# Long convolution by FFT and phase mixing on one core: an inverse table kept on chip by mirror symmetry, a filter spectrum stored once and read doubled, and the phases cut into half tiles, 16 of 44 woven into the last group

## Chip, cores and metric

One core of one Trainium2 chip. The metric is the device time of one execution in microseconds (us), the median of several. All runs told here may be compared. They were made in rounds, on several chips of the machine, and in each round the kernel before ran too. The granted TensorE clock is given as a share of full speed.

## The reference

```python
# x (8, 5696, 128), h (5696, 128), all float32
def _attn_ref(x, h):                       # causal long convolution along the sequence
    L = 2 * S
    y = irfft(rfft(x, n=L, axis=1) * rfft(h, n=L, axis=0)[None], n=L, axis=1)[:, :S]
def _moe_ref(x, w_theta, w_tok_r, w_tok_i, w_ch):   # its x is y of above
    theta = x @ w_theta
    zr, zi = x * cos(theta), x * sin(theta)
    y = einsum('ts,bsd->btd', w_tok_r, zr) + einsum('ts,bsd->btd', w_tok_i, zi)
    u = x + y
    return u + maximum(u @ w_ch, 0)
```

## The kernel before

The FFT of length 11392 is split as 178 x 64. An *evacuation* is the copy of matmul results out of PSUM, the memory into which TensorE accumulates, by VectorE or ScalarE. The program has these parts, in order:

- *Set-up*: trigonometric tables, and the spectrum of h, which goes to HBM. The table of the inverse's last step goes to HBM too.
- *Eight groups* (four pairs of batches, two halves of the 128 channels). Each group has a *middle stage* (C, first inverse step, with A, the first forward step of the next group, interleaved), and then a *forward/inverse stage* (B of the next group interleaved with D of this one). B multiplies by the spectrum of h in 12 chunks; each chunk loads one tile `hs` of 256 KB. Three of these stages (after groups 0, 2 and 4) also load new x, 5.8 MB. The last group has no next one, so its last stage is D alone.
- *Phases*: 22 tiles of 128 tokens, each with theta, sine (made in a tile `red`), cosine (in a tile `mag`) and five stores: one of y, two of zr, two of zi. They load the transposed result back as `ya`.
- *Token pass*: the large matmuls, about 1650 us. The change leaves it alone.

```python
hf_hbm = nc.dram_tensor("hf_hbm", (2, 2 * NCK, P, 2, HD * CK), F16, ...)    # P = 128 rows: every row of 64 twice
e_hbm = nc.dram_tensor("e_hbm", (K1, N2, 2, NB), F16, ...)
fh = pool("fft_h", 3)
# ... set-up: spectrum stored twice (e = 0, 1); seven chunks of the inverse table made and written to e_hbm ...

def stage_b(a_of, dh):                      # forward, second step, and product with the spectrum
    def chunk(c):
        hs = fh.tile([P, 2, HD * CK], F16, tag="hs", name="hs")
        nc.sync.dma_start(hs, hf_hbm[dh, c])
        ps = f2(a_of, c)
        xs = fs.tile([P, 2, HD, CK], F16, tag="xs", name="xs")
        nc.scalar.activation(xs[:, :, :, :ck], ps, AF.Copy)
        for r in range(2):
            nc.vector.tensor_tensor(uv[r][...], xs[...], hv[:, r:r + 1, ...].to_broadcast(...), op=mult)

def stage_c(st):                            # inverse, first step: 16 matmuls a chunk, then
    ...
        nc.vector.tensor_copy(st["g"][...], ps[...])

def stage_d(st, bp, dh):                    # inverse, last step
    def chunk(n0, cn):
        et = fs.tile([P, CN, 2, NB], F16, tag="et", name="et")
        nc.sync.dma_start(et[:K1, :cn], e_hbm[:, n0:n0 + cn, :, :])
        ...
                nc.tensor.matmul(o, g_[:K1, ri * N2 + n0 + j, :], et[:K1, j, ri, :], ...)
        nc.scalar.activation(yt[...], ps[...], AF.Copy)

for g, (bp, dh) in enumerate(groups):
    st = {}
    nxt, a_of = front(g + 1) if g + 1 < len(groups) else ([], None)
    woven(stage_c(st), nxt)
    if dh == 0 and bp + 1 < B // 2:
        x16s[bp + 1] = load_x(bp + 1)
    woven(stage_b(a_of, groups[g + 1][1]) if nxt else [], stage_d(st, bp, dh))

# phases: pool of red and mag with bufs=4; eight loads of ya; then 22 times
#   8 transposes, copies to y_ap (half VectorE, half ScalarE), store of y_ap,
#   theta by matmuls, Abs, Sin, Sin on ScalarE (1024 wide), two products on VectorE,
#   four stores of zr and zi:
        for r, (z, dst) in enumerate(((zr, zr_hbm), (zi, zi_hbm))):
            for e in range(2):
                ...
                nc.sync.dma_start(dst[p_, t0 // 64, i, :, b0 * D:b0 * D + n], z[e * 64:e * 64 + 64])
```

## Time and profile before

Two runs: 2367.80 and 2369.16 us, median 2368.48. The table is read from the trace. "Gap" is the time from the end of a middle stage's last evacuation (1.2 us after its start) to the start of the next middle stage's first one: that is the forward/inverse stage.

| Part | us |
|---|---|
| first middle stage's first evacuation at | 131.5 |
| gaps with x (three) | 39.3, 39.8, 39.3 |
| gaps without x (three), and the last | 28.1, 25.9, 25.0, 24.6 |
| last middle stage's first evacuation at | 562.4 |
| from there to the last phase tile on ScalarE (705.0) | 142.6 |
| rest, the token pass | about 1658 |

The windows view gives busy times by stage. Its columns are the window, its length, then busy us and instruction count of TensorE, its weight loads, VectorE, ScalarE and GpSimd, then the granted TensorE clock, the DMA share (of 16 engines; that it comes out a little over 1 in one row shows that it is rough) and GB/s. The rows are a middle stage, a gap with x, a gap without, the last inverse stage, the wait for ya, and the phases.

```profile
core 0: us, PE busy (x) PEld busy (x) DVE busy (x) ACT busy (x) POOL busy (x), PEclk, DMA share, GB/s
128.00:161.00 33.00, 32.34 (x419) 32.09 (x420) 21.06 (x19) 12.14 (x16) 0.31 (x1) 0.93 0.09 25
161.00:199.00 38.00, 15.66 (x465) 14.18 (x465) 14.51 (x24) 16.63 (x20) 1.84 (x4) 0.71 0.94 213
231.00:256.00 25.00, 15.93 (x457) 14.43 (x455) 14.35 (x24) 16.58 (x20) 0.00 (x0) 0.72 0.78 216
581.00:603.00 22.00, 11.08 (x129) 9.39 (x126) 5.45 (x13) 6.14 (x8) 13.95 (x27) 0.50 1.12 184
603.00:626.00 23.00, 6.49 (x53) 4.41 (x52) 0.42 (x1) 0.29 (x1) 0.00 (x0) 0.61 0.95 238
626.00:709.00 83.00, 54.26 (x577) 38.69 (x574) 68.65 (x84) 77.25 (x88) 0.00 (x0) 0.92 0.90 267
```

The middle stage is TensorE's (32.3 of 33 us). In both gaps no engine is busy for more than 17 us, while the DMA share is 0.78 to 0.94: loads bound them. In the phases ScalarE is busy 77 of 83 us.

The waits view of the eight groups (us in total, times, longest) names those loads: the spectrum tile hs and the inverse table et.

```profile
DVE u_t L274 <- DMA hs<-hf_hbm: 87.5, 36, 16.5
PE ps L305 <- DMA et<-e_hbm: 75.8, 28, 11.1
```

The DMA view of a gap without x (232 to 254 us): GB/s in 40 slices, and the issue line (count, size, median us from issue to landing).

```profile
GB/s 0 117 188 265 140 217 364 275 177 252 322 297 243 198 163 178 201 156 197 276 145 244 150 118 355 333 256 149 30 45 160 264 111 149 293 256 318 198 315 319
hs<-hf_hbm SPq DMA_DIRECT2D x10, 256.0 KB, 4.2
```

An hs of 256 KB landed in 4.2 us while et and the stores of yt ran beside it, and the rate moved mostly between 110 and 360 GB/s.

### The profile page before, as it was taken

Reading aid. Unit: us, or ns where it says so; the run is one execution under the profiler, and the core shown is the slowest. Engines: PE = TensorE matmul, PEld = TensorE weight load, DVE = VectorE, ACT = ScalarE, POOL = GpSimd, SP = SyncE. Lnnn points to the kernel's source line nnn. Section 1 sums busy time; section 2 is a strip of 40 time slices with the busy share of each in tenths; the row PEclk is TensorE's granted clock in tenths of the full one; section 3 lists DMA queues with packets and bytes.
Section 4 is the critical chain, followed back from the end, with each engine's and each line's share of the span. In section 5 each row is a group of like instructions: output and inputs, shape, how many; then the busy total and the mean of one; then the engine's idle time right before and its main releaser. Section 6 shows DMA issues by size and latency. Waiting matters only on the chain.

```text
span 2363.4 us, 42201 instructions
## 1 busy us (share of the span) xinstructions
PE 2068.5 (88%) x16255; PEld 1184.1 (50%) x16255; DVE 1671.0 (71%) x2943; ACT 641.9 (27%) x895; POOL 841.2 (36%) x1527
## 2 busy tenths in 40 slices
PE   3367868686567999999999999799999999999997
PEld 3367768586343444444444444334444444444444
DVE  6555546466387888888787776797677677677774
ACT  6544435453492233322232000001111111111111
POOL 4200000001102544545455655344444544544540
PEclk9578879788789999999999999999999999999998
DMA  4644453645989999989899998977887977977972
GB/s 87 168 97 125 119 145 115 164 115 137 234 271 239 168 173 179 178 155 171 142 184 170 167 148 130 292 106 133 153 140 128 157 138 132 156 135 137 154 130 57
DMA packets 410896, 362.03 MB, mean 153 GB/s; under 512 B 81280, under 2 KB 354858, under 8 KB 408870
## 3 DMA queue, kind: packets, MB, share of 16 engines
q0 software_dynamic: 218240, 143.00, 44.9%
q1 hardware_dynamic: 178055, 197.86, 28.9%
q10 hardware_dynamic: 14400, 18.48, 2.5%
q8 instruction: 127, 2.08, 0.4%
q14 instruction: 74, 0.61, 0.1%
HBM read 398.95 MB, written 103.12 MB: 212 GB/s over the span
## 4 chain that ended last, share of the span: by engine, by line
PE 60%; DMA 4%; DVE 4%; issue 2%; POOL 2%; ACT 2%; ACTq 1%; SPq 0%; DVEq 0%; POOLq 0%
PE m L784 55%; DMA wb<-in_moe_w_tok_r_dram 2%; POOL wb L506 1%; DMA wb<-in_moe_w_tok_i_dram 1%; DVE c L791 1%; PE v L603 1%; PE utp L596 1%; PE m L745 1%; PE m L747 1%; PE m L788 1%; DVE wt L515 1%; ACTq L460 1%; DMA b<-zr_hbm 1%; PE theta_ps L367 0%; PE tpz L545 0%
## 5 line engine op out<-in xcount | busy, mean ns | idle before, releaser
L506 POOL DMA_DIRECT2D wb<-in_moe_w_tok_i_dram x720 | 387.6, 546 | 715.3 <-DVE wt L515 647.2
L506 POOL DMA_DIRECT2D wb<-in_moe_w_tok_r_dram x720 | 386.8, 547 | 388.8 <-DVE wt L515 165.8
L784 PE MATMUL m<-b,wt 128*128 128x512 bf16 x1936 | 456.5, 382 | 8.4 <-DVE wt L515 5.7
L515 DVE STREAM_TRANSPOSE wt<-wb 128x384 f32<-128x384 f32 (+2 forms) x720 | 360.5, 525 | 134.1 <-PE m L784 68.2
L784 PEld LDWEIGHTS <-wt 128*128 128x128 bf16 x1936 | 190.1, 98 | 242.4 <-issue 12.2
L791 DVE TENSOR_TENSOR c<-c,m 128x512 f32<-128x512 f32 x440 | 284.0, 671 | 0.0
L598 ACT ACTIVATE uts<-utp 128x512 bf16<-128x512 bf16 (+1 forms) x90 | 53.3, 592 | 616.1 <-PE utp L596 616.1
L287 PE MATMUL ps<-r_u,u_t 128*128 128x128 f16 x1024 | 143.2, 233 | 41.0 <-DVE u_t L274 40.6
L189 PE MATMUL ps<-f_t,x 89*128 89x88 f16 (+1 forms) x1024 | 145.4, 302 | 36.1 <-ACT a__864 L191 31.6
L189 PEld LDWEIGHTS <-x 89*128 89x128 f16 x1024 | 137.1, 269 | 36.6 <-issue 36.5
L274 DVE TENSOR_TENSOR u_t<-xs,hs 128x1024 f16<-128x1024 f16 x96 | 63.4, 660 | 116.1 <-DMA hs<-hf_hbm 88.2
L288 PE MATMUL ps<-r_v,v_t 128*128 128x128 f16 x1024 | 140.4, 231 | 0.3
L287 PEld LDWEIGHTS <-u_t 128*128 128x128 f16 x1024 | 112.4, 110 | 41.7 <-DVE u_t L274 41.7
L126 POOL DMA_DIRECT2D x<-in_x_dram x16 | 8.4, 534 | 307.9 <-PE ps L189 307.9
L593 ACT ACTIVATE ub<-c 128x512 bf16<-128x512 f32 (+1 forms) x90 | 56.5, 628 | 222.1 <-DMA wb<-in_moe_w_tok_i_dram 158.3
L288 PEld LDWEIGHTS <-v_t 128*128 128x128 f16 x1024 | 108.2, 106 | 2.5 <-DVE v_t L274 1.3
L271 ACT ACTIVATE xs<-ps 128x1024 f16<-128x1024 f32 x96 | 91.7, 975 | 32.6 <-DVE v_t L274 29.0
L547 ACT ACTIVATE yb<-tpz 128x512 bf16<-128x512 bf16 (+1 forms) x46 | 27.4, 597 | 184.5 <-PE tpz L545 132.3
L208 PEld LDWEIGHTS <-w_t 64*128 64x128 f16 x3240 | 63.7, 105 | 17.6 <-issue 12.5
L307 ACT ACTIVATE yt<-ps 128x890 bf16<-128x890 f32 (+1 forms) x56 | 48.0, 858 | 78.9 <-PE ps L305 78.9
L605 DVE SCALAR_TENSOR_TENSOR c<-v,c 128x512 f32<-128x512 f32 (+1 forms) x90 | 61.6, 684 | 11.0 <-PE v L603 10.5
L369 ACT ACTIVATE red<-theta_ps,magic 128x512 f32<-128x512 f32 (+1 forms) x46 | 31.6, 687 | 129.0 <-PE theta_ps L367 100.0
(2845 smaller groups left out, 3810.6 us busy)
## 6 DMA issues: line engine op xcount, KB each, us to landing
wb<-in_moe_w_tok_r_dram POOLq DMA_DIRECT2D x352, 96.0 KB, 4.5
wb<-in_moe_w_tok_i_dram POOLq DMA_DIRECT2D x352, 96.0 KB, 5.0
wb<-in_moe_w_tok_r_dram POOLq DMA_DIRECT2D x352, 80.0 KB, 4.4
wb<-in_moe_w_tok_i_dram POOLq DMA_DIRECT2D x352, 80.0 KB, 3.9
hs<-hf_hbm SPq DMA_DIRECT2D x96, 256.0 KB, 4.2
cp_hbm<-c SPq DMA_DIRECT2D x88, 256.0 KB, 2.2
c<-cp_hbm SPq DMA_DIRECT2D x88, 256.0 KB, 4.6
out_dram<-c SPq DMA_DIRECT2D x88, 256.0 KB, 4.4
```

What stands on the lines that cost most here:

```text
L189: nc.tensor.matmul(ps[:, i // 4, (i % 4) * 2 * kn:(i % 4 + 1) * 2 * kn], lhs(q + i), f1_t[:NB, 2 * k0:2 * k0 + 2 * kn], start=True, stop=True)
L208: nc.tensor.matmul(ps[:, e, j * HD:(j + 1) * HD], w_t2[rows, k0 + c0 + j, N2 * (1 - ri):N2 * (3 - ri)], a_[rows, ri * kn + c0 + j, :], sta ...
L271: nc.scalar.activation(xs[:, :, :, :ck], ps, AF.Copy)
L274: nc.vector.tensor_tensor(uv[r][:, :, :, k0:k0 + ck], xs[:, :, :, :ck], hv[:, r:r + 1, :, :ck].to_broadcast([P, 2, HD, ck]), op=mult)
L287: nc.tensor.matmul(o, u_t[:, at:at + P], r_u, start=True, stop=False)
L288: nc.tensor.matmul(o, v_t[:, at:at + P], r_v, start=False, stop=True)
L506: nc.gpsimd.dma_start(wb[32 * i:32 * i + 32, :ng, :nj * 64], bass.AP(tensor=a.tensor, offset=a.offset + row0 * S + p * H + i * QR + j0 * 6 ...
L515: nc.vector.transpose(wt.rearrange("p j t r -> p (j t r)").bitcast(F32).rearrange("p (j g t) -> p g j t", j=TJ, g=4)[:, :ng, :nj], wb[:, : ...
L593: nc.scalar.activation(ub[:m].rearrange("p b d -> p (b d)"), c[:m], AF.Copy)
L605: nc.vector.scalar_tensor_tensor(c[:m], v[:m], 0.0, c[:m], op0=ALU.max, op1=ALU.add)
L784: nc.tensor.matmul(ms[q], a[q][:, j, :, r], bts[jj][q][:, r, :], start=(jj == 0 and r == 0), stop=(jj == NJ - 1 and r == 1 and q not in left))
L791: nc.vector.tensor_tensor(c, z, ms[q], op=op)
```

## The change

Intent: (1) keep 33 of the 64 rows of the inverse table in on-chip memory and get the rest by reading a row reversed, with signs folded into the evacuation of the middle stage, so that no et is written or loaded; (2) store the spectrum of h once (64 rows) and let each hs load read it twice, by a stride of zero; (3) weave set-up's table chunks into transforms; (4) make the phases 44 half tiles (512 wide), and weave 16 of them into the last group, 10 in its middle stage and 6 in its last one.

```diff
-    hf_hbm = nc.dram_tensor("hf_hbm", (2, 2 * NCK, P, 2, HD * CK), F16, kind="Internal").ap()
+    hf_hbm = nc.dram_tensor("hf_hbm", (2, 2 * NCK, N2, 2, HD * CK), F16, kind="Internal").ap()
-        fh = pool("fft_h", 3)
+    fh = pool("fft_h", 4, conv, side="right")
@@ set-up (cut: tables woven into the transforms, three inverse-table chunks instead of seven)
+        for ri in range(2):
+            nc.sync.dma_start(
+                hf_hbm[:, c, :, ri, :].rearrange("h p n -> p h n"),
+                hst[kh][64 * ri:64 * ri + 64, c % NCK].rearrange("p h d k -> p h (d k)"))
+    e_t = fc.tile([P, EN, 2, NB], F16)          # EN = 33
+    sgn = fc.tile([P, 2, N2], F32)
@@ stage_b
-                nc.sync.dma_start(hs, hf_hbm[dh, c])
+            src = hf_hbm[dh, c]
+            nc.sync.dma_start(hs.rearrange("p r n -> p (r n)"),
+                              bass.AP(tensor=src.tensor, offset=src.offset,
+                                      ap=[[0, 2], [2 * HD * CK, N2], [1, 2 * HD * CK]]))
@@ stage_c
-                nc.vector.tensor_copy(st["g"][...], ps[...])
+            nc.vector.tensor_tensor(st["g"][...], ps[...], sg, op=mult)
@@ stage_d
-                et = fs.tile([P, CN, 2, NB], F16, tag="et", name="et")
-                nc.sync.dma_start(et[:K1, :cn], e_hbm[:, n0:n0 + cn, :, :])
+                    e_ = e_t[:K1, n, ri, :] if n < EN else e_t[:K1, N2 - n, ri, ::-1]
+                    nc.tensor.matmul(o, g_[:K1, ri * N2 + n, :], e_, start=(ri == 0), stop=(ri == 1))
@@ phases
+        sb1 = pool("s2", 2, pha, reuse_waits="tile")        # red, mag: 2 buffers of 512, were 4 of 1024
+    def load_ya(hh):                                        # four batches, four loads on ScalarE's queue
+    def phase_step(ti, hh):                                 # one half tile: y, and four stores of zr and zi
@@ the group loop
+        now = [steps0.pop(0) for _ in range(10)] if last else []
+        woven(stage_c(st), nxt, now)
+        if g + 2 == len(groups):
+            xin.close(); open_phases(); load_ya(0)
+        now = [steps0.pop(0) for _ in range(6)] if last else []
+        woven(stage_b(a_of, groups[g + 1][1]) if nxt else [], stage_d(st, bp, dh), now)
+    load_ya(1)                                              # then the other 28 steps
```

## The prediction

> **What bounds it now.** Median 2368 us. By the windows view the token matmuls (770 us to the end) hold TensorE 98% busy at clock 0.99; the change leaves them alone. The first 770 us have several limits (line and window views):
> - Set-up, 0 to 128 us. In 57 to 110 us the first x transform, about 19 us of work, takes 53: the waits view shows TensorE waiting 31.6 us for ScalarE's evacuations, queued between seven inverse-table chunks and waits for the table's and spectrum's writes (8.4 and 16.1 us). Clock 0.50[...].
> - Forward/inverse stages: 37 to 39 us in the three that also load x, 22 to 25 in the other four. ScalarE is busy 17 us of each; waits are 88 us for hs and 76 us for et in all; DMA share 0.74 to 0.92: DMA-bound.
> - Middle stages, 32 us each: TensorE-bound, unchanged.
> - Last group: 20 us DVE-bound plus 23 us waiting for et at clock 0.50; then 23 us waiting for ya; then phases, 626 to 709 us, 3.43 us per tile, ScalarE-bound.
>
> **Costs and gains.**
> 1. Set-up: three table chunks, no write-back, half the spectrum bytes, tables woven into transforms. First middle stage near 100 us instead of 128.6: -28.
> 2. et gone: 2 of about 6.5 MB per forward/inverse stage. Stages without x drop to ScalarE's 17 us plus bubbles, 18.5 us: -16 over three. Those with x keep the hs starvation behind x (longest wait 16.5 us); one more hs buffer helps little: 31 us, -18 over three. Reading the spectrum doubled leaves the bytes read unchanged. The stage before last also loads half of ya (2.9 MB): +4.
> 3. Warmer clock as middle stages start: -3. The cast becomes a multiply by signs of 1024 PSUM elements: same 1.2 us, by analogy with the f32 adds (512 in 0.67 us). Reversed table read: assumed free.
> 4. Weaving phases. A half tile costs ScalarE about 1.67 us and DVE 1.55, so by engines alone the tail would shrink by 40 us. But each step issues five DMAs on the sync queue whatever its width: the timeline shows 0.53 us for y and 1.09 for each pair of z stores, 3.1 us per tile. Now there are 44 steps instead of 22, and two red/mag buffers instead of four, each held until its store lands (2.6 us): about 3.3 us per step. [...] So: last middle stage with 10 steps 36 us (was 20), last inverse with 6 steps 20 (was 23), other 28 steps 92 (ya wait plus phases were 106). Net about 0, uncertain by 15.
> 5. Start of the token pass: tables and weights share space with the phases, +3.
>
> Sum about -58 us: most from set-up and et, little from the weaving.
>
> **Prediction: 2312 us, 8 in 10 between 2282 and 2338.** Faster by over 2% (below 2321): 0.62; within 2%: 0.36; slower: 0.02.
>
> **What would show it.** First middle stage at 95 to 107 us; no-x forward/inverse stages 18 to 20; x stages 29 to 33; no wait for et; in the phases, steps 3 to 3.5 us apart, the sync queue's issues back to back and ScalarE half idle; phases ending 145 to 160 us after the last forward stage.
>
> **What would make it wrong.** If the sync queue does not pace half tiles, the tail shrinks by 40 us more and the time falls below 2285. If the two-buffer ring or ya's load blocks ScalarE, or the doubled number of 1 KB rows saturates DMA, the tail grows and the result stays within 2%.

(To the clock of point 3: in the trace of the kernel before, the granted clock is 0.50 to 0.73 in the first 3 us of the eight middle stages and 1.00 from 6 us after their start to near their end. The -3 itself is my estimate.)

## The result

The change took 2569.38 us (median of two runs) against 2368.48. A ratio in this document is the mean time of one kernel's runs over the mean of the other's runs of the same rounds, so not quite the ratio of the quoted medians. Here it is 1.0848 (95% interval 1.0802 to 1.0895): 8.5% slower, where 2.4% faster was predicted. Below, runs of different rounds are compared by their medians; taken from the ratios, such differences come out up to some 3 us otherwise. The mean granted clock fell from 0.936 to 0.900.

The windows view of the changed kernel: a middle stage, a gap with x, a gap without, the last middle stage with 10 half tiles, the last inverse stage with 6, and the other 28 steps with the wait for ya. Columns as above.

```profile
131.00:161.00 30.00, 30.00 (x385) 29.95 (x384) 21.80 (x16) 11.67 (x16) 0.00 (x0) 0.96 0.09 32
161.00:224.00 63.00, 16.35 (x503) 14.94 (x495) 15.03 (x25) 16.97 (x20) 2.17 (x4) 0.60 0.33 83
255.00:306.00 51.00, 16.51 (x484) 15.18 (x477) 15.59 (x25) 16.64 (x20) 0.00 (x0) 0.61 0.17 56
737.00:770.00 33.00, 27.53 (x387) 22.92 (x386) 31.76 (x43) 16.18 (x28) 0.00 (x0) 0.99 0.40 98
770.00:788.00 18.00, 13.14 (x195) 10.80 (x192) 9.44 (x18) 13.52 (x21) 0.00 (x0) 0.91 0.45 108
788.00:908.00 120.00, 60.72 (x408) 40.76 (x405) 57.01 (x101) 55.20 (x92) 13.03 (x24) 0.62 0.76 196
```

The engines' work in a gap is what it was (ScalarE 17 us), but the gaps are 63 and 51 us instead of 38 and 25, and the DMA share is not high, it is *low*: 0.17 to 0.33. The waits view of the groups:

```profile
DVE u_t L307 <- DMA hs<-hf_hbm: 261.5, 56, 16.3
ACT xs L304 <- DVE v_t L307: 193.1, 42, 15.8
```

There is no wait for et any more. The wait for hs has grown from 87.5 to 261.5 us, and ScalarE waits behind it. Seen in order of time, VectorE in a gap without x (start, duration, what, and in brackets the idle time before it and what ended it):

```profile
265.62 0.69 DVE L307 TENSOR_TENSOR u_t<-xs,hs 128x1024 f16<-128x1024 f16 x1 [3.37 <-DMA hs<-hf_hbm]
...
281.44 0.69 DVE L307 TENSOR_TENSOR u_t<-xs,hs 128x1024 f16<-128x1024 f16 x1 [3.98 <-DMA hs<-hf_hbm]
...
286.71 0.69 DVE L307 TENSOR_TENSOR u_t<-xs,hs 128x1024 f16<-128x1024 f16 x1 [3.98 <-DMA hs<-hf_hbm]
...
291.99 0.69 DVE L307 TENSOR_TENSOR u_t<-xs,hs 128x1024 f16<-128x1024 f16 x1 [3.98 <-DMA hs<-hf_hbm]
```

Each product starts 5.27 us after the one before, as by a clock. The DMA view of 262 to 298 us, where nothing but hs is under way:

```profile
DMA  1211111111111211111111111111111111111111
GB/s 50 68 55 50 50 50 50 50 50 50 50 50 50 68 46 50 50 50 50 50 50 50 50 50 50 50 48 48 50 50 50 50 50 50 50 50 50 50 50 41
DMA packets 887, 1.82 MB, mean 51 GB/s; under 512 B 14, under 2 KB 14, under 8 KB 884
hs<-hf_hbm SPq DMA_DIRECT2D x7, 256.0 KB
```

A flat 50 GB/s: 262144 bytes in 5.27 us are 49.7 GB/s. The busy share of the 16 engines is a flat tenth; the full line for this queue gives 13.0%, and 2 of 16 is 12.5%. Before, the same transfer ran beside other loads and still landed in 4.2 us.

Only eight of a gap's 12 chunks come at this pace. The first four lie on chip when the gap begins (VectorE multiplies them from 256.3 to 262.3 us). Eight times 5.27 us are about 42 of the 51 us of a gap without x. In a gap with x the fifth chunk waits longer, while x's 5.8 MB are loading, and then steps of 5.27 us follow:

```profile
184.68 0.69 DVE L307 TENSOR_TENSOR u_t<-xs,hs 128x1024 f16<-128x1024 f16 x1 [16.25 <-DMA hs<-hf_hbm]
```

(That the gaps with x, at 63.2, 63.0 and 62.9 us, equal 12 times 5.27 us is chance.)

This is how the time spreads. "Two loads" is the first experiment below.

| us | before | predicted | after | two loads |
|---|---|---|---|---|
| first middle stage at | 131.5 | about 103 | 131.6 | 103.8 |
| gaps with x | 39.3, 39.8, 39.3 | 6 less each | 63.2, 63.0, 62.9 | 31.7, 31.4, 32.3 |
| gaps without x | 28.1, 25.9, 25.0 | 5 less each | 51.7, 51.0, 51.0 | 21.1, 22.8, 21.0 |
| gap before the last group | 24.6 | 4 more | 54.9 | 25.5 |
| last middle stage at | 562.4 | about 501 | 736.9 | 498.0 |
| from there to the last phase | 142.6 | about the same | 164.2 | 165.0 |

The "predicted" column is worked out from the terms of the prediction (562.4 - 28 - 16 - 18 + 4 - 3 = 501).

### The profile page after: what moved, and what is told of

Read it like the earlier page. It is cut to its first block, busy times and chain, and to the rows that moved or that the text cites. A ratio compares the mean times of both kernels' runs of the same rounds, so it can differ in the third digit from the quotient of the medians.

```text
span 2567.6 us, 42483 instructions
## 1 busy us (share of the span) xinstructions
PE 2090.9 (81%) x16255; PEld 1197.2 (47%) x16255; DVE 1695.1 (66%) x3004; ACT 637.8 (25%) x931; POOL 841.8 (33%) x1521
## 4 chain that ended last, share of the span: by engine, by line
PE 55%; DMA 5%; DVE 3%; POOL 2%; issue 1%; ACT 1%; SPq 0%; DVEq 0%; ACTq 0%; POOLq 0%
PE m L814 50%; DMA wb<-in_moe_w_tok_r_dram 2%; POOL wb L536 1%; DMA wb<-in_moe_w_tok_i_dram 1%; DVE c L821 1%; PE utp L626 1%; PE v L633 1%; PE m L775 1%; PE m L777 1%; PE m L818 1%; DMA zr_hbm<-mag 1%; DVE wt L545 1%; DMA y_hbm<-yb 1%; PE theta_ps L377 0%; PE tpz L575 0%
## 5 line engine op out<-in xcount | busy, mean ns | idle before, releaser
L217 PEld LDWEIGHTS <-w_t 64*128 64x128 f16 x3240 | 69.0, 108 | 72.7 <-issue 49.5
L307 DVE TENSOR_TENSOR v_t<-xs,hs 128x1024 f16<-128x1024 f16 x96 | 64.8, 675 | 0.0
```

The lines of the kernel that those rows point to most:

```text
L217: nc.tensor.matmul(ps[:, e, j * HD:(j + 1) * HD], w_t2[rows, k0 + c0 + j, N2 * (1 - ri):N2 * (3 - ri)], a_[rows, ri * kn + c0 + j, :], sta ...
L307: nc.vector.tensor_tensor(uv[r][:, :, :, k0:k0 + ck], xs[:, :, :, :ck], hv[:, r:r + 1, :, :ck].to_broadcast([P, 2, HD, ck]), op=mult)
```

## The experiments

The theory, after the result: the doubled read runs on two of the 16 DMA engines. For this speak the 13.0% of the 16 engines' time above, where 2 of 16 is 12.5%, and the flat 50 GB/s. What is new in the form of the load is the repeat of two, now its slowest dimension; that this 2 is what gives two engines was a supposition, which the experiment with a 4 below tests. The rivals: reading the same HBM rows twice at nearly the same time is slow whatever the engines; or it is something else of the change, such as the order of the loads or the smaller stores.

### Two loads of 64 rows

```diff
-            nc.sync.dma_start(hs.rearrange("p r n -> p (r n)"),
-                              bass.AP(..., ap=[[0, 2], [2 * HD * CK, N2], [1, 2 * HD * CK]]))
+            for e in range(2):
+                nc.sync.dma_start(hs[64 * e:64 * e + 64], src)
```

> Edit: the changed kernel, but each hs tile is filled by two plain DMAs of 64 partitions (128 KB) instead of one DMA whose source has a leading repeat dimension of 2. Theory (two engines): the repeated source is spread over only 2 of the 16 DMA engines, so 256 KB take 5.27 us; with two plain loads hs lands in about 4 us, the DMA share of the forward/inverse stages rises from 0.1-0.2 to 0.6-0.9, stages without x take 18-20 us (were 50), those with x 29-33 (were 62), first middle stage at 100 us (was 131), time 2312 us (2290 to 2340). Rival 1 (reading the same 64 stored rows twice is slow in HBM): the same rows are still read twice, so above 2500 us. Rival 2 (the loss is in the woven phases, the sign multiply or the reversed table): above 2500 us, hs waits unchanged.

Measured: 2324.55 us, ratio 0.9818 to the kernel before (0.9804 to 0.9833): faster, but by less than 2%. The spectrum is still stored once, the same rows are still read twice, and the bytes are the same; only the form of the access pattern differs. The stages fell to the table's last column (those without x a little above the 18 to 20 us expected). The wait for hs, 261.5 us in the changed kernel, is down to this:

```profile
DVE u_t L306 <- DMA hs<-hf_hbm: 43.5, 12, 12.0
```

The difference to the changed kernel up to the last middle stage is 736.9 - 498.0 = 238.9 us of 244.8 in all, and it lies where hs is read: 27.8 us in set-up (which ends with the first 12 chunks), 93.7 in the gaps with x, 88.8 in those without, 29.4 in the last one. The rival of rows read twice falls.

The windows view of this kernel: a gap with x, a gap without, the last middle stage, and 26 of the 28 remaining steps, those after the wait for ya.

```profile
134.00:165.00 31.00, 17.11 (x473) 15.61 (x472) 14.40 (x24) 16.02 (x20) 1.72 (x4) 0.71 0.88 190
195.00:216.00 21.00, 15.30 (x510) 14.06 (x507) 15.72 (x25) 16.56 (x20) 0.00 (x0) 0.91 0.54 148
498.00:532.00 34.00, 27.49 (x376) 22.95 (x381) 31.58 (x42) 16.05 (x27) 0.00 (x0) 0.99 0.49 119
577.00:668.00 91.00, 48.83 (x326) 33.50 (x331) 48.41 (x86) 47.28 (x78) 0.00 (x0) 0.65 0.65 176
```

The last row is the next question: in 91 us no engine is busy for much more than half the time.

### The spectrum stored twice again

```diff
-    hf_hbm = nc.dram_tensor("hf_hbm", (2, 2 * NCK, N2, 2, HD * CK), F16, ...)
+    hf_hbm = nc.dram_tensor("hf_hbm", (2, 2 * NCK, P, 2, HD * CK), F16, ...)
-            nc.sync.dma_start(hf_hbm[:, c, :, ri, :] ...)
+            for e in range(2):
+                nc.sync.dma_start(hf_hbm[:, c, 64 * e:64 * e + 64, ri, :] ...)
-            nc.sync.dma_start(hs..., bass.AP(..., ap=[[0, 2], ...]))
+            nc.sync.dma_start(hs, src)
```

> Edit: the changed kernel, but the spectrum is stored twice as before and each hs tile loaded by one plain 128-partition DMA. Theory (two engines): within 10 us of e1_two_loads (2312), up to 5 us slower for 3 MB more of stores at set-up, up to 5 us faster for half the load issues. Rival 1 (same rows read twice): clearly faster than e1_two_loads, which stays above 2500. Rival 2 (not the hs loads): above 2500 us.

Measured: 2325.28 us, ratio 0.9828 (0.9811 to 0.9845), the same as two loads. Its first middle stage comes 2.4 us later (106.2 against 103.8). So one load of 128 rows and two of 64 are equally good, and storing the spectrum once is worth nearly nothing by itself.

### The kernel before with the doubled read alone

```diff
-    hf_hbm = nc.dram_tensor("hf_hbm", (2, 2 * NCK, P, 2, HD * CK), F16, ...)
+    hf_hbm = nc.dram_tensor("hf_hbm", (2, 2 * NCK, N2, 2, HD * CK), F16, ...)
-                nc.sync.dma_start(hs, hf_hbm[dh, c])
+                nc.sync.dma_start(hs..., bass.AP(..., ap=[[0, 2], [2 * HD * CK, N2], [1, 2 * HD * CK]]))
```

> Edit: the kernel before, with only the spectrum stored once and read with the leading repeat of 2. Theory (two engines): 12 loads of 5.27 us = 63 us per group bound all eight forward stages: those with x 62 us (37), without x 51 (24), the first about 50 (18): about 2570 us, hs steps 5.27 us apart. Rival 1 gives the same. Rival 2 (loss elsewhere): 2368 us within 1%.

Measured: 2645.68 us, ratio 1.1173 (1.1154 to 1.1192). The step alone makes the kernel before 11.7% slower, more than expected. Its gaps are 73.7 to 75.1 us with x and 60.1 to 61.0 without. The waits view shows two waits now: VectorE for hs, 339 us, and TensorE for et, 193 us. The et loads are issued from the same sync queue as hs, and an issue of hs in the doubled form lasts 5.08 us there (median, in the changed kernel) instead of 0.32. That et is held behind such issues is inferred from this: no run moved et to another queue, so that part of the excess is not isolated.

### Four engines instead of two

If the two engines come from the 2 of the slowest dimension, a 4 there must double the rate. A gap row after every 16 keeps the four groups of 16 apart in the pattern; a 4 without the gap was not tried. (The stores had to be cut into pieces of 16 partitions for it.)

```diff
-    hf_hbm = nc.dram_tensor("hf_hbm", (2, 2 * NCK, N2, 2, HD * CK), F16, ...)
+    hf_hbm = nc.dram_tensor("hf_hbm", (2, 2 * NCK, 4, 17, 2, HD * CK), F16, ...)
             for e in range(2):
-                nc.sync.dma_start(hs[64 * e:64 * e + 64], src)
+                nc.sync.dma_start(hs[64 * e:64 * e + 64]...,
+                                  bass.AP(..., ap=[[17 * row, 4], [row, 16], [1, row]]))
```

> Edit: e1_two_loads, with the stored spectrum's 64 rows laid out as four groups of 16 with a gap after each, so that each 64-partition load has a source whose slowest dimension is 4 (no repeat, each stored row read by two loads as in e1_two_loads). Theory[...]: 4 engines, 256 KB in half of 5.27 us, 2.6 us, wherever hs is waited for; stages without x about 26 us (21.5 in e1_two_loads, 50 in the changed kernel), those with x 36 to 40; 2350 to 2400 us. Rival 1 (the repeat, stride 0 or the same rows within one DMA, is what is slow, not the size of that dimension): within 10 us of e1_two_loads (2324.6).

Measured: 2415.27 us, ratio 1.0190 (1.0171 to 1.021), a little above the range expected: the first middle stage came at 122.2 instead of 103.8 us (set-up ends with 12 such reads too; the expectation named only the stages), the gaps are 42.8 to 43.3 us with x and 30.0 to 30.9 without, 20 to 22 us shorter than in the changed kernel, where eight times 2.63 would be 21. The sharp part of the expectation held. VectorE in a gap without x:

```profile
244.32 0.69 DVE L310 TENSOR_TENSOR u_t<-xs,hs 128x1024 f16<-128x1024 f16 x1 [1.34 <-DMA hs<-hf_hbm]
...
246.95 0.69 DVE L310 TENSOR_TENSOR u_t<-xs,hs 128x1024 f16<-128x1024 f16 x1 [1.34 <-DMA hs<-hf_hbm]
...
249.59 0.70 DVE L310 TENSOR_TENSOR u_t<-xs,hs 128x1024 f16<-128x1024 f16 x1 [1.34 <-DMA hs<-hf_hbm]
```

The step is 2.64 us, half of 5.27: 99.5 GB/s. Two engines gave 49.7, four 99.5; either way 24.9 GB/s for each engine. A stride of zero is not needed for it: this pattern repeats nothing, and the rate of an engine is the same.

Up to here the number of engines is inferred from rates and shares. In this version, too, the share fits: the busy share of the 16 engines is two tenths in all slices but one from 237 to 249 us, where it was one tenth in the changed kernel; 4 of 16 is 25%. A second sign are the packets under 512 bytes that the DMA view counts: 14 for seven loads in the changed kernel (its line is above), so two for each; in the packet records of its trace they have 4 bytes and come in pairs, at most 7 ns apart, a pair every 5.22 to 5.28 us. In this version (237 to 253 us) there are four for each of twelve, and with two plain loads (195 to 216 us) about 15 for each of 20, if the two stores of yt in that window are left out of account:

```profile
DMA packets 867, 2.15 MB, mean 134 GB/s; under 512 B 48, under 2 KB 48, under 8 KB 817
hs<-hf_hbm SPq DMA_DIRECT2D x12, 128.0 KB
DMA packets 1572, 3.10 MB, mean 148 GB/s; under 512 B 304, under 2 KB 304, under 8 KB 1520
```

I read them as one for each engine at work. And in the packet records of the changed kernel's trace, which no view prints, exactly two packets of 2048 bytes are under way for 92% of the time from 284 to 297 us; a packet takes 85 ns (median). So sizes of 2 and 4 went with two and four engines; other small sizes were not run.

### The mended version without weaving

The rest of the experiments ask why the mended version (two loads) is 22 us slower than the kernel before from the last middle stage to the last phase (165.0 against 142.6), where about no difference was predicted.

```diff
-        now = [steps0.pop(0) for _ in range(10)] if last else []
+        now = []
-        now = [steps0.pop(0) for _ in range(6)] if last else []
+        now = []
```

> Edit: e1_two_loads with none of the phase steps woven into the last group; all 44 half-tile steps follow it. Theory (the sync queue's five issues pace a half tile at 3.1 to 3.5 us): last middle stage 20 us instead of 36, last inverse stage 13 instead of 20, then 44 x 3.2 = 141 us of steps instead of 92: about 26 us slower than e1_two_loads. Rival (engines pace a half tile at 1.7 us): about 5 us slower only.

Measured: 2353.01 us, ratio 0.9940 (0.9925 to 0.9955), 28.5 us slower than with weaving. From the last middle stage to the last phase it takes 188.0 us instead of 165.0. Weaving works: it is worth 23 us there.

### Old phases, not woven

Two loads, with the phases of the kernel before: 22 whole tiles, four buffers, all of ya loaded afterwards, nothing woven. (The diff replaces the phases by the old code.)

> Edit: e1_two_loads, with the last group and the phases as in the kernel before (nothing woven, full-width tiles, 22 steps, four buffers, ya loaded after the last group). Theory (e1_two_loads started its last middle stage 62 us earlier than before, 498 against 560.5 us, but ends only 43 us earlier, so weaving half tiles costs about 19 us): 2305 us (2297 to 2313), 19 us faster than e1_two_loads. Rival (weaving pays, as it was meant to): slower than e1_two_loads.

Measured: 2298.35 us, ratio 0.9717 (0.97 to 0.9735), 26 us *faster* than two loads. The last stretch takes 134.7 us. So half tiles (with their two buffers and their two loads of ya, which were not taken apart here) cost 188.0 - 134.7 = 53 us when nothing is woven, and weaving gives 23 back: the fourth part of the change is a net loss of 30 us in this stretch. The gain over the kernel before there (142.6) is 8 us; the last inverse stage no longer waits for et.

### Why half tiles are slow: two of the five stores on another queue

Each phase step issues five stores from the sync queue, whatever its width. The sync queue of the kernel before (start, time of the issues in us, count), one whole tile:

```profile
641.10 0.53 SPq L474 DMA_DIRECT2D y_hbm<-y_ap  x1
641.73 1.09 SPq L404 DMA_DIRECT2D zr_hbm<-mag  x2
642.87 1.24 SPq L404 DMA_DIRECT2D zi_hbm<-red  x2
644.20 0.54 SPq L474 DMA_DIRECT2D y_hbm<-y_ap  x1
```

And of the two-load version, nine issues (two half tiles have ten):

```profile
591.70 1.18 SPq L413 DMA_DIRECT2D zr_hbm<-mag  x2
592.93 0.59 SPq L413 DMA_DIRECT2D zi_hbm<-red  x1
593.57 1.07 SPq L452 DMA_DIRECT2D y_hbm<-y_ap  x2
594.74 1.09 SPq L413 DMA_DIRECT2D zi_hbm<-red  x2
595.92 1.19 SPq L413 DMA_DIRECT2D zr_hbm<-mag  x2
```

Both are back to back, at some 0.6 us an issue, and both need 3.1 to 3.3 us per step. But a half tile does half the work in it: the steps of the two-load version start 3.33 us apart (586.40 to 663.02, 23 intervals).

```diff
-                nc.sync.dma_start(dst[...], z[e * 64:e * 64 + 64])
+                (nc.gpsimd if r == 1 and turns is not None else nc.sync).dma_start(dst[...], z[e * 64:e * 64 + 64])
```

> Edit: e1_two_loads, with the zi stores of the half-tile steps issued from GpSimd's queue; zr and y stay on the sync queue. In e1_two_loads the last 28 steps come 3.1 to 4 us apart. Theory (sync queue issues pace them): its part falls from five issues (2.9 us) to three (1.8 us) per step, but with two red/mag buffers each step then waits for its store to land at about 3 us: 8 to 20 us faster than e1_two_loads (2324.6). Rival A (only the ring of two buffers paces): no faster than 5 us. Rival B (1 KB rows saturate the DMA engines): no faster.

Measured: 2308.35 us, ratio 0.9756 (0.974 to 0.9772), 16 us faster than two loads. The last stretch fell from 165.0 to 154.1 us, steady steps to 3.04 us. The stores and their bytes are the same, so the sync queue's issuing was part of the pace.

### Four buffers instead of two, and both together

```diff
+    sides["phases"]["sb1"] = pool("s2b", 4, pha, reuse_waits="tile")     # before the 28 remaining steps
     load_ya(1)
```

Four buffers from the start do not fit on chip: the build fails, since half of ya then needs 22 KB in each partition and 17.7 are left. So the four come only after the last group.

> Edit: e1_two_loads, with four red/mag buffers instead of two for the 28 steps after the last group. Theory (sync queue issues pace them): 0 to 10 us faster than e1_two_loads, steps still at least 3.0 us apart. Rival A (ring of two paces): steps 1.7 to 2.2 us apart, 35 us faster. Rival B (DMA engines saturated): no faster.

> Edit: both edits of e4_stores_split and e5_four_bufs. Theory (issues, with the ring just behind): steps 1.9 to 2.3 us apart, 25 to 45 us faster than e1_two_loads, 2280 to 2300 us, the fastest so far. Rival B (DMA engines saturated by 1 KB rows): within 10 us of e1_two_loads.

Measured: four buffers alone 2333.41 us, ratio 0.9870 (0.9845 to 0.9894), 9 us *slower* than two loads; with the stores split too 2304.10, ratio 0.9737 (0.9719 to 0.9754), 20 us faster, where 25 to 45 were expected. The last stretches are 170.4 and 150.4 us. Alone the larger ring moves nothing: the steps stay 3.33 us apart (589.52 to 665.97, 23 intervals), because it is not the pace. That this version is slower still goes with ScalarE's one wait for ya, which grew from 11.2 to 19.9 us; why it grew was not tested. Together they take away both limits, and the steps come 2.03 us apart (588.90 to 603.10) until VectorE fills up: in 603 to 646 us it is busy 34.4 of 43 us, and in the 20 us from 620 to 640 for 19.0. It has the products of the phases, and sums for the token pass which have come due (20 of them, of five kinds, of which one is shown). VectorE, those 43 us (busy us and mean ns):

```profile
L402 DVE TENSOR_TENSOR red<-red,y_ap 128x512 bf16<-128x512 f32 x14 | 9.7, 690 | 7.7 <-ACT red L397 7.7
L500 DVE TENSOR_TENSOR b<-b 128x1024 bf16<-128x1024 bf16 x4 | 2.8, 688 | 0.1
```

### Half of ya loaded ahead, with old phases

From here on the base is "old phases". Batches 0 to 3 of ya are loaded at the start of the last group (with old phases the DMA share is 0.07 from 501 to 520 us there and 0.36 from 520 to 538), batches 4 to 7 at the old place.

```diff
+        if g + 1 == len(groups):
+            ya0 = pool("s2a0", 1, pha, reuse_waits="tile").tile([P, 4, H], BF16, name="ya0")
+            for p_ in range(4):
+                nc.scalar.dma_start(ya0[:, :, p_ * QR:p_ * QR + QR], yt_hbm[:, 0:4, p_ * QR:p_ * QR + QR])
-            nc.scalar.dma_start(ya[:, :, ...], yt_hbm[:, :, ...])
+            nc.scalar.dma_start(ya1[:, :, ...], yt_hbm[:, 4:8, ...])
```

> Edit: e8_old_phases, with the half of ya that belongs to batches 0 to 3 (2.9 MB) loaded at the start of the last group, where the DMA engines were 23% busy, and only the other half after it. Theory: of the 23 us wait for ya before the phases about 10 go: 2285 to 2292 us, 8 to 12 us faster than e8_old_phases (2298.4).

Measured: 2293.23 us, ratio 0.9683 (0.9668 to 0.9697): 5 us better than old phases by the medians, 8 by the ratios, at best the least that was expected, and not for the reason expected. From the last middle stage to the last phase it takes 135.8 us against 134.7: loading half of ya ahead shortened nothing. The 5 us were already there at the last middle stage (496.1 against 501.2), where the edit does nothing; that mark lies between 495.6 and 501.2 in seven versions with the same groups. Why the half load is not faster is taken up in the last experiment.

### Six buffers of hs

```diff
-    fh = pool("fft_h", 4, conv, side="right")
+    fh = pool("fft_h", 6, conv, side="right")
```

> Edit: e9_half_ahead, with six hs buffers instead of four. Theory (in the three stages that load x, hs is starved behind x for about 11 us, and each chunk fetched ahead moves 1.4 us of work before the gap): 3 us less in each of the three, 6 to 10 us faster than e9_half_ahead. Rival (the end of the x load itself bounds these stages): no faster than 3 us.

Measured: 2280.12 us, ratio 0.9626 (0.9612 to 0.9641), 13 us better than with four, more than expected. The gaps with x fell from 31.7, 31.9, 32.8 to 28.3, 28.7, 29.6 us, and the one before the last group from 25.3 to 19.7. I read it so: more chunks are on chip before the load of x is under way. The longest wait for hs came down to 9.0 us (12.0 with two loads, 16.5 in the kernel before). This version beats both kernels: 3.7% under the kernel before, and 2280.12 / 2569.38 = 0.887 of the changed one by medians.

### The second half of ya issued from two queues

In all versions with whole tiles ScalarE's first phase came at once after its eight issues of ya, so I suspected that ScalarE was held by its own issuing.

```diff
-            nc.scalar.dma_start(ya1[:, :, ...], yt_hbm[:, 4:8, ...])
+            (nc.scalar if p_ % 2 else nc.sync).dma_start(ya1[:, :, ...], yt_hbm[:, 4:8, ...])
```

> The six-buffer version, with four of the eight loads of the second half of ya issued on the sync queue and four on ScalarE's. In every version so far ScalarE's first phase comes within 0.6 us of the end of its eight issues: 611.11 + 14.56 then 626.20 in the kernel before, 538.52 + 17.93 then 556.99 with whole tiles, 517.97 + 13.94 then 532.45 with six buffers; half the bytes did not shorten it. Theory: ScalarE is held by its own issuing, in order, and not by the landing of the data. Then four issues take 7 us and the first phase comes at 525 to 527 instead of 532.5; 5 to 8 us faster than the six-buffer version, ratio to the kernel before 0.9595 to 0.961. Rival: [...]the data's landing sets the start: no gain, first phase at 530 to 533, ratio 0.962 to 0.9635.

Measured: 2278.01 us, ratio 0.9628 (0.9609 to 0.9648): the same as six buffers, as the rival said, though the first phase came at 528.1, between the two expectations. (The last middle stage came 2.6 us later here, at 480.6 against 478.0. Counted from there, the first phase came 7.0 us earlier, as the theory said, and the last phase 2.3.) ScalarE with six buffers, and then with the issues split:

```profile
517.97 13.94 ACTq L531 DMA_DIRECT2D ya<-yt_hbm  x8
532.45 1.02 ACT L396 ACTIVATE mag<-theta_ps 128x1024 f32<-128x1024 f32 x1
```

```profile
519.75 4.77 ACTq L531 DMA_DIRECT2D ya<-yt_hbm  x4
528.07 1.02 ACT L396 ACTIVATE mag<-theta_ps 128x1024 f32<-128x1024 f32 x1 [0.22 <-PE theta_ps L393]
534.39 1.02 ACT L396 ACTIVATE mag<-theta_ps 128x1024 f32<-128x1024 f32 x1 [2.36 <-PE theta_ps L393]
```

The issues were quick and the first phase came 4.4 us earlier, but the second had to wait, and the last came at 614.2 us against 613.9. TensorE waits 20.5 us for ya with six buffers and 17.4 with the issues split. With the issues split ScalarE has issued by 524.5 us and starts at 527.3, so there the data's landing sets the start. The DMA engines are full there: the DMA view of 512 to 545 us shows nine tenths or more in every slice from 518 to 539 us, and in this stretch the queue that loads the token pass's first weights takes 45.4% of the 16 engines' time, beside ya and the other queues. That the weights are what keeps the halved ya load from being quicker fits these numbers, but no run moved them away, so it stays open.

## Why the prediction was wrong, point by point

- **The step that failed** is in point 2: "Reading the spectrum doubled leaves the bytes read unchanged." It is true, and it was taken as a cost of nothing. I costed the load by bytes and by the DMA share, and not by the number of engines that it would run on in its new form. The read ran on two of 16 engines (13.0% of their time), 5.27 us for each hs, and turned gaps that were bound by all of the DMA's bandwidth into gaps bound by one slow load at a DMA share of 0.17. Undoing this alone takes 244.8 us off and lands at 2324.55, inside the range predicted; putting it alone into the kernel before costs 11.7%; four engines double the rate. The prediction names no measured time of a load of this form.
- The list of "what would make it wrong" had the sync queue, the ring, ya's load and saturated DMA; the cause was the opposite of saturation. And 0.02 for slower was far too sure for a change with a new form of load in it.
- *Set-up, -28.* Right once the read is mended: 131.5 to 103.8, or -27.7. In the change itself it was eaten whole (131.6), since set-up ends with 12 such reads, for which VectorE waits 28.8 us.
- *et gone: -16 without x, -18 with x, +4 for ya, -3 for the clock.* Right in mechanism and nearly in size: with two loads the gaps without x lost 14 us in sum, those with x 23, and the one before the last group grew by 0.9, where 4 was predicted. Up to the last middle stage 61 us were predicted and 64.4 measured (562.4 - 498.0). Of the -3 for the clock little is seen: the granted clock in a gap without x rose from 0.72 to 0.91, but the seven middle stages before the last became only 0.5 us shorter in all. The remark that "one more hs buffer helps little" was not tested for four against three, but six against four is worth 13 us, so hs starvation behind x was worth more than I gave it.
- *Signs at "same 1.2 us".* A little off: the medians with two loads are 1.29 to 1.43 us beside interleaved forward work, and 1.21 alone, against 1.22 before. The middle stage stays TensorE's and does not feel it.
- *Reversed table read free.* Right: the matmuls take 202 to 286 ns, median 204, with the stored table before, and 200 to 282, median 204, with half of the rows reversed after (first group).
- *Weaving "net about 0, uncertain by 15".* The mechanism was right and the size was off. The last two stages were predicted at 36 and 20 us and took about 34 and 19, and the steps at 3.3 us took 3.33. But "28 steps 92" took about 117 us (551 to 668), of which 24 are three waits of ScalarE where the woven part hands over to the rest: 7.4 us for the landing of a store, 11.2 for ya, 5.7 for a store again. I had taken ya to be hidden by the early half. Net loss in this stretch against the kernel before: 22 us. Against old phases in the same groups it is 30, the sum of +53 for half tiles and -23 for weaving.
- *Start of the token pass, +3.* Nearly right: from the last phase to the end it takes 1660.5 us with two loads, 1658.4 before. The profiled runs differ by 40 us: the 64 gained up to the last middle stage, less these 22 and 2. The prediction had 58.

What stays open: whether a held sync queue is what makes et suffer in the kernel before with the doubled read, why ya is waited for longer with four buffers, what bounds the last load of ya, and what holds an issue. Eight loads of ya, 352 KB each, took 13.94 us to issue from one queue, and four of the same took 4.77 and 3.09 us from two; one issue of hs took 5.08 us (median) in the changed kernel, with two engines at work, and 0.32 in the kernel before.

## What to carry to other kernels

Ask of each new load not only how many bytes it moves but what the outermost dimension of its source is, and measure it when that is small: a repeat of two in front left 14 of 16 DMA engines idle here (a share of 13.0%), a four gave twice the rate (99.5 GB/s against 49.7), and with two plain loads the kernel took no longer than with one of 128 rows (2324.55 us against 2325.28). A wait at a low DMA share (0.17) with a flat GB/s line (50) was its mark. When work is cut into smaller steps, count what each step pays whatever its size, such as issues on one queue, before counting what the overlap brings.
